# A long-convolution and feed-forward kernel: transposes in the network as products with the identity, in two halves of 64 output columns

## The chip, the cores and the metric

The kernel runs on one NeuronCore of a Trainium2 chip. The metric is the device time of one execution in microseconds. A TensorE (PE) instruction pair is one weight load (LDWEIGHTS, shown as PEld) and one product (MATMUL, shown as PE); VectorE is DVE, ScalarE is ACT, GpSimd is POOL.

## The reference

Everything is float32. The first part gates `x` with a long causal convolution of `x * v`; the second is a two-layer network on the 49920 rows that come out.

```python
# B, S, D = 4, 12480, 128
h_mlp = np.maximum(pos_emb @ w1, 0.0) @ w2
h_filt = h_mlp * np.exp(-0.01 * np.arange(S))[:, None]
u = x * v
L = 2 * S
y = irfft(rfft(u, L, axis=1) * rfft(h_filt, L, axis=0)[None], L, axis=1)[:, :S]
rows = (x * y).reshape(B * S, D)
h = rows @ w_in            # w_in 128 x 2048
g = h * np.cos(h)
out = g @ w_out            # w_out 2048 x 128
```

## The kernel before

**Start.** The filter is built, the transforms of the filter and of the first batch are made, and `w_in` and `w_out` are brought into their working form. The transforms are products with tables of sines and cosines in two stages, of 96 and 120 points; `f1`, `f2` and `i1`, `i2` are the forward and inverse stages in the names of the functions.

**The network and the convolution, interleaved.** From line 1114 on (`tiled[0] = True`) one order, written out by hand, mixes two streams on every engine. One stream is the network: 98 tiles (`NALL`) of up to 512 rows each, and per tile 16 chunks (`NFC`) of 128 hidden columns. The other is the convolution of the batches, a generator from which `convolve()` takes a step about once in a chunk; it makes the rows that the network later reads. After about 2970 us only the network is left.

**A chunk.** `moe_up` multiplies the tile's transposed input `at` with a chunk of `w_in` into a PSUM bank `ph` (three of them). ACT (L870), DVE (L871), ACT (L876) and DVE (L877) make `h * cos(h)` of it in `gt`. For two chunks together POOL makes sums of the parts (`ts`, L885 to L889), so that seven products take the place of eight in `moe_down` (L902), which runs seven chunks behind (`LAG = 7`) and adds into the accumulators `acca` and `accb`.

**A tile's transposes.** There are eight in a tile, all issued at chunk `AT = 10` (at the start and the end of the network the groups stand alone).

- `moe_back` takes the sums `ot` of the tile before, as `moe_evict` left them, and turns four blocks of 128x128 into a `ph` bank; `moe_rows` copies that bank to SBUF on ACT (L937), and `moe_store` sends it out.
- `moe_turn` takes the rows `zb` of the next tile (shown in the trace as `tile`), as `moe_load` brought them in, and turns four blocks of 128x128 into a bank of the convolution (`cv`, three banks, two while the first batch lasts); ACT copies it to `at` (L857).

In the order of PE they follow one another: a `moe_down`, then in many tiles a step of the convolution, the four of `moe_back`, the four of `moe_turn`, and then a `moe_up`.

**Two forms on TensorE.** `mm` (L135) issues every product of the network and of the convolution's later stages. Once `tiled[0]` is set it cuts a product in two at output column `CB = 64`, so that one half of the array's columns makes output partitions 0 to 63 and the other half 64 to 127. The products of `moe_down` (L902) and `f1_mm` (L458) are cut in the same way by hand. `transpose` (L140) does not use `mm`: it issues the transposing form over all 128 columns, with the data as the stationary operand and the identity as the moving one. `filter_turn` at the start uses it too, before `tiled[0]` is set.

The tile framework derives the waits between engines from the tiles that are written and read; the order on each engine is the order of issue.

Of the kernel before, what the change touches and what calls it, by code (L numbers as in the profile page):

```python
# [34 lines left out]
def kernel(  # L35
# [46 lines left out]
    nc = tc.nc  # L82
# [50 lines left out]
    tiled = [False]  # L133

    def mm(dst, left, right, start=True, stop=True):  # L135
        n = dst.shape[0]
        for lo, hi in ((0, CB), (CB, n)) if tiled[0] else ((0, n),):
            nc.tensor.matmul(dst[lo:hi], left[:, lo:hi], right, start=start, stop=stop)  # L138

    def transpose(dst, src, ident):  # L140
        n = src.shape[0]
        nc.tensor.transpose(dst, src, ident[0:n, 0:n])  # L142


    def float32_begin(pool, raw):
# [230 lines left out]
    def filter_turn(pool, bank, pe, ident):  # L376
        pt = bank()
        for q in range(ROWS // 2):
            transpose(pt[:, q * 2 * H:(q + 1) * 2 * H], pe[:, q, :], ident)
        peT = pool.tile([P, ROWS * H], F32, name="peT", bufs=3)  # L380
        nc.scalar.copy(out=peT[:, :], in_=pt[:, 0:ROWS * H])
        return peT
# [467 lines left out]
    def moe_turn(pool, n):  # L850
        m = rows_of(n)
        zb = zbs.pop(n)
        pt = bank()
        for i in range(G):
            transpose(pt[:, i * m:(i + 1) * m], zb[0:m, i, :], ident)
        at = pool.tile([D, BANK], F32, name="at")
        nc.scalar.copy(out=at[:, 0:G * m], in_=pt[:, 0:G * m])  # L857
        ats[n] = at
# [67 lines left out]
    def moe_back(n, ot):  # L926
        m = rows_of(n)
        pt = ps_h.tile([P, BANK], F32, name="ph")
        places = pt[:, :].rearrange("p (h i e d) -> p h e i d", h=2, e=2, d=CB)
        for i, block in enumerate((1, 2, 3, 0)):  # L930
            transpose(places[0:m, i // 2, i % 2], ot[:, block, 0:m], ident)
        return pt
# [21 lines left out]
    with tc.manual_schedule():  # L954
        with tc.tile_pool(name="psum", bufs=8, space=PSUM) as psum, \
# [15 lines left out]
            with tc.tile_pool(name="layers", bufs=1, side="right") as pool:  # L971
# [31 lines left out]
                ident = pool.tile([P, P], F32, name="ident")  # L1003
# [68 lines left out]
            ident = wpool.tile([P, P], F32, name="ident")  # L1072
# [61 lines left out]
        for i in range(len(steps) + LAG):  # L1134
# [5 lines left out]
            if i < len(steps):  # L1140
                n, c = steps[i]
# [55 lines left out]
```

## Time and profile before

| | |
|---|---|
| median of 3 runs | 3618.33 us (3617.26 to 3621.39) |
| profiled execution, device time | 3616.25 us |
| its span | 3614.5 us |
| PE busy | 3567.7 us, 99% of the span |
| DVE, POOL, ACT busy | 2836.4, 2752.1, 2234.2 us (78%, 76%, 62%) |
| mean share of DMA engines | 26.2% for the main queue |
| granted TensorE clock | 0.999 of full |
| transposes in the network (L142) | 784: 392 into `ph`, 392 into `cv` |
| chain that ended last | PE 84%, DVE 4%, POOL 2% |

A float32 product is recorded as two LDWEIGHTS and MATMUL pairs, so a product cut in two halves leaves four MATMUL records; a transpose in the transposing form leaves one. Matmuls are pipelined: a record lasts longer than the distance to the next one's start, so costs on PE are read from starts, not from durations. A line of the order-of-time view gives the start in us, the time from the first start to the last end of a run of like instructions, engine, line, operation, tiles written and read, shape, and the count of records.

### The profile page before, as it was taken

Reading aid. Unit: us, or ns where it says so; the run is one execution under the profiler, and the core shown is the slowest. Engines: PE = TensorE matmul, PEld = TensorE weight load, DVE = VectorE, ACT = ScalarE, POOL = GpSimd, SP = SyncE. Lnnn points to the kernel's source line nnn. Section 1 sums busy time; section 2 is a strip of 40 time slices with the busy share of each in tenths; the row PEclk is TensorE's granted clock in tenths of the full one; section 3 lists DMA queues with packets and bytes.
Section 4 is the critical chain, followed back from the end, with each engine's and each line's share of the span. In section 5 each row is a group of like instructions: output and inputs, shape, how many; then the busy total and the mean of one; then the engine's idle time right before and its main releaser. Section 6 shows DMA issues by size and latency. Waiting matters only on the chain.

```text
span 3614.5 us, 102269 instructions
## 1 busy us (share of the span) xinstructions
PE 3567.7 (99%) x40830; PEld 2533.1 (70%) x40830; DVE 2836.4 (78%) x5289; ACT 2234.2 (62%) x4482; POOL 2752.1 (76%) x3240
## 2 busy tenths in 40 slices
PE   8999999999999999999999999999999999999999
PEld 7996767666677767666677776766667776666666
DVE  7888885688887885688887786588887667877877
ACT  7776766666654556665655556665655446676676
POOL 7777985688855895698864897588885458878877
PEclk9999999999999999999999999999999999999999
DMA  6545530122214640122202551022220350000000
GB/s 189 157 147 169 159 114 16 35 72 70 70 35 130 171 134 13 31 71 72 76 26 68 171 171 47 13 65 72 74 63 15 109 153 19 19 25 19 19 23 17
DMA packets 224195, 281.85 MB, mean 78 GB/s; under 512 B 23386, under 2 KB 161122, under 8 KB 223594
## 3 DMA queue, kind: packets, MB, share of 16 engines
q1 hardware_dynamic: 223722, 275.30, 26.2%
q8 instruction: 326, 5.34, 0.6%
q14 instruction: 147, 1.20, 0.1%
HBM read 194.75 MB, written 80.46 MB: 76 GB/s over the span
## 4 chain that ended last, share of the span: by engine, by line
PE 84%; DVE 4%; POOL 2%; issue 1%; ACT 1%; DMA 0%; POOLq 0%; ACTq 0%; SPq 0%; DVEq 0%
PE ph L138 31%; PE accb L902 17%; PE cv L138 17%; PE acca L902 13%; PE cv L458 3%; DVE gt L871 1%; DVE gt L877 1%; PE ph L142 1%; PE cv L142 1%; ACT gt L870 1%; POOL ts L885 1%; POOL slots L450 0%; POOL ts L888 0%; DVE t L517 0%; DVE xt L440 0%
## 5 line engine op out<-in xcount | busy, mean ns | idle before, releaser
L871 DVE SCALAR_TENSOR_TENSOR gt<-ph,gt 128x512 f32<-128x512 f32 (+1 forms) x1380 | 948.9, 688 | 680.0 <-ACT gt L870 674.9
L870 ACT ACTIVATE gt<-ph 128x512 int32<-128x512 f32 (+1 forms) x1380 | 822.8, 596 | 1056.7 <-PE ph L138 992.6
L138 PE MATMUL ph<-at,w_in_sb 128*64 128x512 f32 (+1 forms) x5520 | 1429.0, 593 | 7.7 <-DVE gt L877 6.1
L885 POOL TENSOR_TENSOR ts<-gt 128x512 f32<-128x512 f32 (+2 forms) x784 | 1001.3, 1277 | 569.8 <-PE accb L902 565.6
L876 ACT ACTIVATE gt<-gt 128x512 f32<-128x512 f32 (+1 forms) x1568 | 972.3, 620 | 6.7 <-DVE gt L871 5.3
L877 DVE TENSOR_TENSOR gt<-ph,gt 128x512 f32<-128x512 f32 (+1 forms) x1380 | 936.6, 679 | 0.0
L902 PE MATMUL accb<-ts,w_out_sb 128*64 128x128 f32 (+2 forms) x9408 | 650.0, 272 | 0.0
L889 POOL TENSOR_TENSOR ts<-gt,ts 128x256 f32<-128x256 f32 (+2 forms) x784 | 575.7, 734 | 61.5
L888 POOL TENSOR_TENSOR ts<-ts,gt 128x256 f32<-128x256 f32 (+2 forms) x784 | 575.5, 734 | 61.4
L902 PEld LDWEIGHTS acca<-gt,w_out_sb 128*64 128x64 f32 x6272 | 395.4, 136 | 262.9 <-issue 228.6
L902 PEld LDWEIGHTS accb<-ts,w_out_sb 128*64 128x64 f32 x9408 | 543.7, 137 | 0.0
L902 PE MATMUL acca<-gt,w_out_sb 128*64 128x128 f32 (+2 forms) x6272 | 477.8, 272 | 0.0
L902 PEld LDWEIGHTS accb<-gt,w_out_sb 128*64 128x64 f32 x3136 | 221.4, 136 | 251.7 <-issue 198.7
L138 PEld LDWEIGHTS ph<-at,w_in_sb 128*64 128x64 f32 x5520 | 345.9, 137 | 37.7 <-issue 17.7
L902 PE MATMUL accb<-gt,w_out_sb 128*64 128x128 f32 (+1 forms) x3136 | 310.5, 273 | 4.9 <-DVE ot L923 3.3
L138 PEld LDWEIGHTS cv<-slots,tm 96*40 96x40 f32 (+1 forms) x3840 | 226.4, 125 | 119.5 <-issue 112.3
L902 PE MATMUL acca<-ts,w_out_sb 128*64 128x128 f32 (+1 forms) x3136 | 307.5, 272 | 1.5 <-POOL ts L888 1.4
L518 POOL TENSOR_TENSOR slots<-slots,t 120x256 f32<-120x256 f32 x288 | 210.7, 733 | 72.8 <-DVE t L517 62.0
L138 PE MATMUL cv<-slots,tm 96*40 96x128 f32 (+1 forms) x3840 | 253.0, 273 | 3.4 <-DVE slots L564 3.4
L138 PEld LDWEIGHTS cv<-even,slots 120*64 120x64 f32 (+1 forms) x3072 | 165.7, 125 | 65.0 <-issue 60.2
L902 PEld LDWEIGHTS acca<-ts,w_out_sb 128*64 128x64 f32 x3136 | 200.4, 137 | 2.5 <-POOL ts L888 2.3
L138 PE MATMUL cv<-at,w_in_sb 128*64 128x512 f32 (+1 forms) x752 | 191.7, 586 | 0.0
(140 smaller groups left out, 3834.8 us busy)
## 6 DMA issues: line engine op xcount, KB each, us to landing
h<-hd SPq DMA_DIRECT2D x144, 240.0 KB
tm<-td SPq DMA_DIRECT2D x96, 312.0 KB
xt<-in_x_dram SPq DMA_DIRECT2D x120, 208.0 KB
xs<-in_x_dram SPq DMA_DIRECT2D x120, 208.0 KB
zd<-xs SPq DMA_DIRECT2D x119, 208.0 KB
tile<-zd SPq DMA_DIRECT2D x96, 256.0 KB
vt<-in_v_dram SPq DMA_DIRECT2D x90, 208.0 KB
w<-wd SPq DMA_DIRECT2D x144, 105.0 KB
```

Of the source, the lines that this page charges most:

```text
L138: nc.tensor.matmul(dst[lo:hi], left[:, lo:hi], right, start=start, stop=stop)
L142: nc.tensor.transpose(dst, src, ident[0:n, 0:n])
L458: nc.tensor.matmul(dst[lo:hi], u[:, b, lo:hi, i], c1[0:u.shape[0], r:r + 2, :].rearrange("p r k -> p (r k)"), start=True, stop=True)
L518: nc.gpsimd.tensor_tensor(y[:, r], y[:, r], t[:, r], op=op)
L870: nc.scalar.activation(turns, ph[:, 0:m], AF.Identity, bias=phase)
L871: nc.vector.scalar_tensor_tensor(out=part, in0=ph[:, 0:m], scalar=phase, in1=turns, op0=ALU.add, op1=ALU.subtract)
L876: nc.scalar.activation(part, part, AF.Sin, scale=scale)
L877: nc.vector.tensor_tensor(part, ph, part, op=ALU.mult)
L885: nc.gpsimd.tensor_tensor(ts[:, 0:2, 0:half], gt[:, :, half:2 * half], gt[:, 0, 0:2 * half].rearrange("p (h n) -> p h n", h=2), op=ALU.sub ...
L888: nc.gpsimd.tensor_tensor(t[2], t[1], b11, op=ALU.add)
L889: nc.gpsimd.tensor_tensor(t[3], b21, t[2], op=ALU.subtract)
L902: nc.tensor.matmul(acc[h * CB:(h + 1) * CB, place, 0:r], w_out_sb[:, pair, weight, :], right[:, h * r:(h + 1) * r], start=(pair == 0 and i ...
```

## The change

In the network (when `tiled[0]` is set) `transpose` calls `mm` with the same data as the stationary operand and the same identity as the moving one. The product is cut at output column 64 as all others. Before the network, in `filter_turn`, the transposing form stays. Nothing else is touched: the order, the banks and the copies on ACT are the same.

```diff
     def transpose(dst, src, ident):
         n = src.shape[0]
-        nc.tensor.transpose(dst, src, ident[0:n, 0:n])
+        if tiled[0]:
+            mm(dst, src, ident[0:n, 0:n])
+        else:
+            nc.tensor.transpose(dst, src, ident[0:n, 0:n])
```

## The prediction

> **What bounds the kernel now.** I read the page first: the shares by engine and the chain that ended last.
>
> ```profile
> span 3614.5 us, 102269 instructions
> PE 3567.7 (99%) x40830; PEld 2533.1 (70%) x40830; DVE 2836.4 (78%) x5289; ACT 2234.2 (62%) x4482; POOL 2752.1 (76%) x3240
> ...
> PE 84%; DVE 4%; POOL 2%; issue 1%; ACT 1%; DMA 0%; POOLq 0%; ACTq 0%; SPq 0%; DVEq 0%
> ```
>
> PE is the bound: 99% busy, 84% of the chain. A busy PE is not yet a PE without slack, so I asked for busy times by stage, and show a stage in which the convolution's products with the spectrum run beside the network (690 to 1010 us, one of three alike) and the last one, network alone.
>
> ```profile
> 690.00:1010.00 320.00, 318.31 (x3352) 202.46 (x3350) 277.52 (x547) 192.79 (x352) 282.09 (x332) 1.00 0.24 69
> 2970.00:3572.00 602.00, 600.75 (x6503) 388.58 (x6503) 477.38 (x792) 419.35 (x769) 482.70 (x528) 1.00 0.07 21
> ```
>
> The columns are the length, then busy us of PE, PEld, DVE, ACT and POOL, the granted clock, the DMA share and GB/s. PE is without idle time in both. In the first, DVE (277.5 of 320) and POOL (282.1 of 320) are near it, 87 and 88%; in the second they are at 79 and 80%. So a microsecond added to PE is a microsecond of the span, but for places where PE waits today for DVE. Those I looked for last, in the groups of the transposes by form.
>
> ```profile
> L142 PE MATMUL ph<-ident,ot 128*128 128x128 f32 x384 | 62.9, 286 | 1.0 <-DVE gt L877 1.0
> L142 PE MATMUL cv<-ident,tile 128*128 128x128 f32 x384 | 58.2, 274 | 6.8 <-DVE t L517 4.2 <-PE ph L142 1.5 <-issue 1.1
> ```
>
> 384 records are 96 tiles of four: one record for each transpose. Ahead of `moe_turn`'s four PE sat idle 6.8 us in the whole run, mostly for a `cv` bank that DVE's L517 still read.
>
> **The change, step by step.** The cost comes from starts in the order of time on PE, here around one tile's eight transposes.
>
> ```profile
> 2018.33 0.61 PE L902 MATMUL acca<-gt,w_out_sb 128*64 128x128 f32 x8
> 2018.77 0.39 PE L902 MATMUL acca<-ts,w_out_sb 128*64 128x128 f32 x4
> 2018.99 1.03 PE L138 MATMUL ph<-at,w_in_sb 128*64 128x512 f32 x4
> 2019.84 1.07 PE L138 MATMUL cv<-slots,tm 96*64 96x128 f32 x16
> ...
> 2025.18 0.82 PE L902 MATMUL accb<-ts,w_out_sb 128*64 128x128 f32 x12
> 2025.93 0.66 PE L142 MATMUL ph<-ident,ot 128*128 128x128 f32 x4
> 2026.42 0.60 PE L142 MATMUL cv<-ident,tile 128*128 128x128 f32 x4
> 2026.95 1.08 PE L138 MATMUL ph<-at,w_in_sb 128*64 128x512 f32 x4
> 2027.86 0.61 PE L902 MATMUL acca<-gt,w_out_sb 128*64 128x128 f32 x8
> ```
>
> *Price of a product in halves.* The first two lines: 8 records from 2018.33 to 2018.77, 4 more to 2018.99. Four records are one product with 128 moving columns in two halves, so it takes 0.22 us of PE; the median over all runs of four such L902 starts is 0.218. L902 is as near as a row can be: 128 contracted rows, 64 output columns a half, 128 moving columns, new float32 weights for each. The convolution's 96-row product takes the same (16 records in 0.91 us at 2019.84, 0.22 each), so the rows do not set the price. The new transpose is this product: eight in a tile take 8 x 0.218 = 1.744 us.
>
> *What is taken out.* Eight transposes from 2025.93 to 2026.95: 1.02 us. Inside a group they start 0.109 us apart, half the product's price. But the group also pays at its edges. The twelve L902 records should hold PE for 3 x 0.218 = 0.654 us, to 2025.83; the first transpose starts at 2025.93: 0.10 us lost. Of the 1.02 us, 8 x 0.109 = 0.87 is streaming, and the other 0.15 lies after the first and the last transpose. The `ph` product behind takes 0.91 us (2026.95 to 2027.86) where the one at 2018.99 takes 0.85 to 0.86: 0.05 lost. So the eight cost 0.10 + 1.02 + 0.05 = 1.17 us, of which 0.30 is the price of going from halves to the whole array and back. Is that 0.30 the array's, or a wait that would stay? In 22 of the tiles the first transpose waits for no semaphore at all, and its start still stands 0.20 us behind the last L902 start, where 0.10 to 0.11 is usual. So I take it to go away with the form.
>
> The Trainium skill, "TensorEngine Tiling (Array Packing)", section Tiling Modes, says that changing the tiling mode drains TensorE. The 0.30 us agrees with it, and by that rule alone the change would be a gain of 98 x 0.30 = 29 us. The same skill's "Perfetto Trace Analysis", section Transposes, says that a transpose should use the transposing form and not an ordinary matmul; the steps of 0.218 against 0.109 us agree with that. The rows price both, and the second is the larger.
>
> *Net for a tile with PE at work throughout:* 1.744 - 1.17 = +0.575 us. 96 tiles: +55.2 us. Four groups stand alone (two `moe_turn` at the start, two `moe_back` at the end): 4 x 0.218 - (4 x 0.109 + 0.30) = +0.14 us each, 0.6 together. Sum +55.8 us.
>
> *What hides some of it.* Where PE waits at `moe_turn`'s bank, a longer `moe_back` eats the wait:
>
> ```profile
> 761.32 0.64 PE L138 MATMUL cv<-slots,w 124*64 124x256 f32 x4
> 761.88 0.66 PE L142 MATMUL ph<-ident,ot 128*128 128x128 f32 x4
> 762.97 0.66 PE L142 MATMUL cv<-ident,tile 128*128 128x128 f32 x4 [0.43 <-DVE t L517]
> 763.56 1.08 PE L138 MATMUL ph<-at,w_in_sb 128*64 128x512 f32 x4
> ```
>
> Here the second group starts 1.09 us after the first, not 0.49. With products the first group starts 0.10 earlier and takes 0.872, so it is done 0.77 after today's start: of the 0.60 us of waiting 0.28 is eaten. Counting in the order of time, 18 of the 96 paired blocks take over 1.1 us in place of 1.02: 18 x 0.27 = 4.9 us at most. The seven tiles from 280 to 540 us stand in a stage where PE is idle 10 us for other waits too (DVE's L877 ahead of `ph`); there I let the other 0.29 us be hidden as well: 2 us. Bounds: nothing hidden, 0; all of PE's idle time in the network hidden, by stages 10 (280 to 540 us), 14 (540 to 3572) and 6 (the end), 30 us. I take 7, near the lower end, because the waits that the trace names at these blocks are that small.
>
> *What comes at no cost.* ACT waits for the longer groups (L857, L937) and everything queued behind it on ACT (the next L870, L876) moves back by the same 0.58 us; but PE's next `ph`, which feeds them, moves back as much, so no bank comes later relative to PE. DVE and POOL get 0.58 us of slack in each tile. If that cover failed and ACT's lag came back to PE in full, it would cost as much again, 0.58 us a tile or 55 us; today's waits show PE held by ACT at `ph` once, for 0.6 us. Weight loads: four of 64 columns for one of 128. L902 streams the same load per product at 0.218 us, so they are inside that price. No DMA is added; 784 x 3 = 2352 more pairs, 5.8% of PE's 40830, come with the same density as L902's.
>
> *Sum.* 55.8 - 7 = +48.8 us on the profiled execution's 3616.25 (span 3614.5 and 1.75 around it). The median of the runs, 3618.33, lies 2.08 higher; I add to that: 3667.
>
> **Rivals.**
>
> *A gain: one pass is enough.* The transposing form leaves one record and starts every 0.109 us; if a product with the identity also went at 0.109 us, only the 0.30 us of switching would be left of the account: 98 x -0.30 = -29 us, 3589. The point of decision is a price per product of 1.17 / 8 = 0.146 us. For it: the switch is real, and the transposing form shows that a 128-column pass can start every 0.109 us. Against it: every L902 product with 128 columns leaves four records at 0.218, and no row of a float32 product with 128 moving columns is near 0.146. 5%.
>
> *The switch price stays.* If the 0.30 us came from the banks changing hands or from waits on PE's own semaphore, and not from the form, the change costs 0.30 x 98 = 29 us more: 3697. For it: 24 of the first transposes wait for PE's own semaphore. Against it: the 22 that don't wait. Half of the ACT lag above coming back to PE would give the same time. 6%.
>
> *The halves do not run side by side.* Then a product costs 0.436, a tile 8 x 0.436 - 1.17 = +2.3 us, 228 in all: 3846. Against it: L902's and L138's halves start 5 ns apart throughout, and L138's use one moving operand for both halves, as here. 2%.
>
> *More is hidden than I count,* up to the 30 us: 3644. For it: DVE and POOL at 87 and 88% in three stages, which the slack lets catch up. Against it: the order of time shows PE's waits at the transposes in 18 tiles alone, and in the last 600 us, 22 tiles, PE has nothing to hide behind. Values down to 3654 belong to my forecast, below that 5%.
>
> **Chances and range.** Forecast, slower by about 49 us: 82%, with 3654 (20 us hidden) to 3674 (nothing hidden) as its own ends. The rest as above. The range reaches from 3654 past the uncovered sum towards the case in which a third of the switch price stays (10 us): 3654 to 3684. A measurement of this kernel can tell 0.2%, 7 us, from no change. Slower by over that: all but the gain and a sliver left for the unforeseen, 0.94; within it 0.01; faster 0.05.
>
> **What would show it.** Right: L142 `ph` and `cv` records in the network become four for each transpose, 64 columns wide, at 0.218 us a transpose; the block of eight takes 1.74 us; the first starts 0.10 to 0.11 us after the last L902 record; the `ph` product behind takes 0.86; the last stage, 22 tiles, grows by 22 x 0.575 = 12.6 us; PE's idle time at `moe_turn` shrinks. Wrong: groups of eight at under 1.17 us (the gain), a start 0.20 us behind L902 as today (the switch stays), or starts of the two halves 0.1 us apart (no overlap).

## The result and the profile after

The median is 3669.40 us (3668.72 to 3670.05, four runs) against 3619.24 us before (3617.26 to 3621.39, four runs): 50.2 us slower, a ratio of 1.0138 (95% interval 1.0121 to 1.0156). The profiled execution took 3668.97 us, its span 3667.2 us, 52.7 us above the span before. Three parts of the page say where PE stands: its head, the shares by engine, and the chain that ended last.

```profile
span 3667.2 us, 106973 instructions
PE 3626.0 (99%) x43182; PEld 2690.7 (73%) x43182; DVE 2827.2 (77%) x5289; ACT 2224.6 (61%) x4482; POOL 2748.6 (75%) x3240
...
PE 86%; DVE 4%; POOL 1%; ACT 1%; issue 1%; DMA 0%; ACTq 0%; POOLq 0%; DVEq 0%
```

PE is busy 58.3 us longer, with 2352 more MATMUL records; DVE, ACT and POOL do the same work in a longer span. The transposes of the network now belong to `mm` (L138), here in the groups by form:

```profile
L138 PE MATMUL ph<-ident,ot 128*64 128x128 f32 x1552 | 105.0, 273 | 1.5 <-DVE gt L880 1.0 <-DVE ot L926 0.4
L138 PE MATMUL cv<-ident,tile 128*64 128x128 f32 x1536 | 102.8, 273 | 4.1 <-issue 2.2 <-DVE t L520 1.3 <-PE ph L138 0.6
```

1536 records are 96 tiles of four transposes of four records each; the `ph` form holds 16 more, the first halves of the short tiles. Idle time ahead of `moe_turn`'s group fell from 6.8 to 4.1 us, the part that DVE ended from 4.2 to 1.3. The order of time on PE shows the same tile that the prediction took apart, `moe_back`'s group first:

```profile
2050.00 0.39 PE L905 MATMUL accb<-gt,w_out_sb 128*64 128x128 f32 x4
2050.22 0.82 PE L905 MATMUL accb<-ts,w_out_sb 128*64 128x128 f32 x12
2050.87 1.04 PE L138 MATMUL ph<-ident,ot 128*64 128x128 f32 x16
2051.74 1.04 PE L138 MATMUL cv<-ident,tile 128*64 128x128 f32 x16
2052.62 1.03 PE L138 MATMUL ph<-at,w_in_sb 128*64 128x512 f32 x4
2053.47 0.39 PE L905 MATMUL acca<-gt,w_out_sb 128*64 128x128 f32 x4
```

Starts 2050.87, 2051.74 and 2052.62 make four transposes 0.87 us, 0.218 each. The first starts 0.65 us behind the twelve L905 records, which is what these take; the 0.10 us of before is gone. The `ph` product takes 0.85 us, not 0.91.

The tile that waited for `moe_turn`'s bank:

```profile
767.43 1.05 PE L138 MATMUL ph<-ident,ot 128*64 128x128 f32 x16
768.64 1.09 PE L138 MATMUL cv<-ident,tile 128*64 128x128 f32 x16 [0.16 <-DVE t L520]
```

The second group starts 1.21 us after the first, and 0.87 of that is work: 0.34 us of waiting is left of the 0.60 before.

**A finer measure.** Where the network runs alone, the distance from one tile to the next repeats to a few ns, so a price can be read there without the noise of whole runs. I take it from the starts of ACT's copy into `at`; two of them after the change are

```profile
3205.32 0.59 ACT L860 COPY at<-cv 128x512 f32<-128x512 f32 x1 [1.50 <-PE cv L138]
3233.29 0.59 ACT L860 COPY at<-cv 128x512 f32<-128x512 f32 x1 [1.50 <-PE cv L138]
```

27.97 us apart; before the change the median of twenty is 27.411, after it 27.971, +0.560 us. The experiments below are compared by this, beside their medians.

### The profile page after: what moved, and what is told of

Same layout as the page of the kernel before. It is cut to its first block, busy times and chain, and to the rows that moved or that the text cites. A ratio compares the mean times of both kernels' runs of the same rounds, so it can differ in the third digit from the quotient of the medians.

```text
span 3667.2 us, 106973 instructions
## 1 busy us (share of the span) xinstructions
PE 3626.0 (99%) x43182; PEld 2690.7 (73%) x43182; DVE 2827.2 (77%) x5289; ACT 2224.6 (61%) x4482; POOL 2748.6 (75%) x3240
## 4 chain that ended last, share of the span: by engine, by line
PE 86%; DVE 4%; POOL 1%; ACT 1%; issue 1%; DMA 0%; ACTq 0%; POOLq 0%; DVEq 0%
PE ph L138 33%; PE cv L138 19%; PE accb L905 17%; PE acca L905 13%; PE cv L461 3%; DVE gt L874 1%; DVE gt L880 1%; ACT gt L873 1%; POOL ts L888 0%; POOL slots L453 0%; DVE t L520 0%; DVE xt L443 0%; POOL ts L891 0%; DVE slots L518 0%; DVE slots L567 0%
## 5 line engine op out<-in xcount | busy, mean ns | idle before, releaser
L138 PE MATMUL ph<-at,w_in_sb 128*64 128x512 f32 (+1 forms) x5520 | 1444.5, 592 | 5.1 <-DVE gt L880 4.1
L905 PE MATMUL accb<-ts,w_out_sb 128*64 128x128 f32 (+2 forms) x9408 | 661.2, 272 | 0.0
L905 PEld LDWEIGHTS acca<-gt,w_out_sb 128*64 128x64 f32 x6272 | 417.2, 136 | 244.2 <-issue 214.2
L905 PEld LDWEIGHTS accb<-ts,w_out_sb 128*64 128x64 f32 x9408 | 554.8, 137 | 0.0
L905 PE MATMUL acca<-gt,w_out_sb 128*64 128x128 f32 (+2 forms) x6272 | 490.5, 272 | 0.0
L905 PEld LDWEIGHTS accb<-gt,w_out_sb 128*64 128x64 f32 x3136 | 240.5, 136 | 235.7 <-issue 186.8
L138 PEld LDWEIGHTS ph<-at,w_in_sb 128*64 128x64 f32 x5520 | 370.4, 137 | 18.2 <-DVE gt L880 7.7
L905 PE MATMUL accb<-gt,w_out_sb 128*64 128x128 f32 (+1 forms) x3136 | 321.8, 273 | 4.1 <-DVE ot L926 2.8
L905 PE MATMUL acca<-ts,w_out_sb 128*64 128x128 f32 (+1 forms) x3136 | 320.1, 272 | 1.3 <-POOL ts L891 1.2
L138 PEld LDWEIGHTS cv<-slots,tm 96*40 96x40 f32 (+1 forms) x3840 | 227.9, 125 | 120.2 <-issue 112.4
L138 PE MATMUL cv<-slots,tm 96*40 96x128 f32 (+1 forms) x3840 | 254.2, 273 | 4.4 <-DVE slots L567 3.4
L905 PEld LDWEIGHTS acca<-ts,w_out_sb 128*64 128x64 f32 x3136 | 212.9, 137 | 2.3 <-POOL ts L891 2.1
L138 PEld LDWEIGHTS cv<-even,slots 120*64 120x64 f32 (+1 forms) x3072 | 165.7, 125 | 65.0 <-issue 60.1
L461 PEld LDWEIGHTS cv<-c,slots 104*64 104x64 f32 (+1 forms) x1536 | 140.9, 137 | 85.0 <-issue 66.6
```

The lines of the kernel that those rows point to most:

```text
L461: nc.tensor.matmul(dst[lo:hi], u[:, b, lo:hi, i], c1[0:u.shape[0], r:r + 2, :].rearrange("p r k -> p (r k)"), start=True, stop=True)
L905: nc.tensor.matmul(acc[h * CB:(h + 1) * CB, place, 0:r], w_out_sb[:, pair, weight, :], right[:, h * r:(h + 1) * r], start=(pair == 0 and i ...
```

## The experiments

The theory: PE sets the time; a product costs 0.218 us, a transposing form 0.109, and going from halves to the whole array and back costs 0.30 us once for a block. The change pays the first difference eight times and saves the last once. Rivals: the edges cost nothing, or belong to the transposing form and not to the width, or the forecast was met by errors that cancel.

**1. Products over the whole array** (`e1_whole`)

```diff
         if tiled[0]:
-            mm(dst, src, ident[0:n, 0:n])
+            nc.tensor.matmul(dst, src, ident[0:n, 0:n], start=True, stop=True)
```

> Transposes as ordinary products with the identity, but over all 128 output columns, not in two halves. Theory (0.30 us at the edges of a tile's block is the price of going from halves to the whole array and back, whatever the form): the edge price stays and each transpose costs 0.218 us in place of 0.109, so +0.87 us a tile; 27.41 us a tile in the network's last stage becomes 28.28; 85 us in all, some 7 hidden, about 3697 us against 3619 before. Rival (the edge price belongs to the transposing form): as the changed kernel, 27.97 us a tile, about 3669 us.

3703.78 us, ratio to before 1.0239 (1.0222 to 1.0256); 28.367 us a tile. The order of time on PE in the last stage:

```profile
3316.40 0.85 PE L905 MATMUL accb<-ts,w_out_sb 128*64 128x128 f32 x12
3317.18 1.16 PE L143 MATMUL ph<-ident,ot 128*128 128x128 f32 x8
3318.18 1.06 PE L143 MATMUL cv<-ident,tile 128*128 128x128 f32 x8
3319.16 1.08 PE L138 MATMUL ph<-at,w_in_sb 128*64 128x512 f32 x4
3320.07 0.61 PE L905 MATMUL acca<-gt,w_out_sb 128*64 128x128 f32 x8
```

The edges are back with no transposing form in the block: the twelve records hold PE for 0.655 us, and the first product starts 0.78 us behind their start; `ph` takes 0.91. So the price goes with the width of the array, and the rival falls. The kernel is 7 us slower than expected, 0.085 us a tile: inside a group the products start every 0.223 us, not 0.218, and the second record of the block starts 0.21 us behind the first, 0.05 more than in the kernel before.

**2 and 3. One of the two groups alone** (`e2_back_only`, `e3_turn_only`)

```diff
-    def transpose(dst, src, ident):
+    def transpose(dst, src, ident, halves=False):
...
-        if tiled[0]:
+        if halves:
             mm(dst, src, ident[0:n, 0:n])
...
# e2: halves=True in moe_back's call; e3: in moe_turn's
```

> Only moe_back's four transposes become products in halves; moe_turn's keep the transposing form. Theory: the array still goes to the whole width and back once in a tile, so the 0.30 us stays and four transposes cost 0.109 more: +0.436 us a tile, 27.85 us in the last stage; 42.7 us in all, less about 6 that the longer first group hides of the waits for moe_turn's bank: about 3655 us. Rival (no price at the edges, the cost simply goes with the number of products): half of the 50 us, 27.69 us a tile, about 3644 us.

> Only moe_turn's four transposes become products in halves; moe_back's keep the transposing form. Theory: +0.436 us a tile, 27.85 us in the last stage, 42.7 us in all, and since the longer group comes behind the wait for the bank, little is hidden (up to 2 us): about 3660 us, some 5 more than with moe_back alone; the two together exceed the whole change's 50 us by the price of one change of width, about 28 us. Rival (no price at the edges): half of the 50 us, about 3644 us.

3654.57 us (ratio 1.0103, 1.0088 to 1.0118) and 3656.75 us (1.0110, 1.0095 to 1.0125), against 3617.27 us of the kernel before beside them: +37.3 and +39.5. In the last stage 27.846 and 27.849 us a tile, +0.435 and +0.438, where the rival gave 27.69. The parts add to 0.873, the whole change is 0.560: 0.313 us a tile is paid by each part and not by the whole, the change of width. Of the order between the two by what is hidden, the medians show 2 us where 5 were expected, which is within their intervals (some 5 us to each side). The single traces agree better: the last copy into `at` stands 37.1 us later than before in e2 and 41.1 in e3.

**4. The two groups apart, in the transposing form** (`e4_apart`)

```diff
-                if c == (AT if n else NFC - 2) and n + 1 < NALL:
-                    moe_turn(mpool, n + 1)
                 ...
                 hidden[i] = moe_up(mpool, n, c, pairs[i - c % 2], ph)
+                if c == (AT if n else NFC - 2) and n + 1 < NALL:
+                    moe_turn(mpool, n + 1)
```

> The kernel before, with moe_turn's four transposes issued behind the chunk's moe_up, so that a product in halves lies between the two groups: twice from halves to the whole array and back in a tile. Theory: +0.30 us a tile, 27.71 us in the last stage (22 tiles, +6.6 us); in all +29 us less up to 10 us of waits for moe_turn's bank that the later place avoids: 3638 to 3648 us. Rival (the edges cost nothing, the place alone counts): the last stage stays at 27.41 us a tile and the run at 3609 to 3619 us.

3671.30 us, ratio 1.0150 (1.0135 to 1.0165): the last stage as expected, 27.711 us a tile, exactly +0.300; the whole run 54 us slower where 19 to 29 were expected. From tile 8 to 12 (553 to 699 us before) a tile cost +0.50 us, from tile 12 to 22 (699 to 1018) +0.71. ACT in order of time, between 553 and 699 us, suggests a cause:

```profile
593.63 0.59 ACT L937 COPY tile<-ph 128x512 f32<-128x512 f32 x1 [2.06 <-PE cv L142]
594.11 0.60 ACT L870 ACTIVATE gt<-ph 128x512 int32<-128x512 f32 x1
594.60 0.59 ACT L857 COPY at<-cv 128x512 f32<-128x512 f32 x1
595.07 0.65 ACT L876 ACTIVATE gt<-gt 128x512 f32<-128x512 f32 x1
```

and PE beside it:

```profile
591.29 0.66 PE L142 MATMUL ph<-ident,ot 128*128 128x128 f32 x4
591.88 1.08 PE L138 MATMUL ph<-at,w_in_sb 128*64 128x512 f32 x4
592.89 0.66 PE L142 MATMUL cv<-ident,tile 128*128 128x128 f32 x4
593.48 0.66 PE L902 MATMUL acca<-gt,w_out_sb 128*64 128x128 f32 x8
593.97 0.39 PE L902 MATMUL acca<-ts,w_out_sb 128*64 128x128 f32 x4
594.27 1.08 PE L138 MATMUL ph<-at,w_in_sb 128*64 128x512 f32 x4
```

L937 copies the bank that `moe_back` filled by 591.95, yet it starts at 593.63, released by `moe_turn`'s group on `cv`. It writes `tile`, the one buffer that also holds the rows which `moe_turn` reads. All that is queued behind it on ACT waits too. PE's next `ph` product, due 0.22 us after 593.97, starts at 594.27, 0.08 us late and just behind the end of L937 (593.63 + 0.59), which still read one of the three `ph` banks. In the waits by pairs, PE's `ph` behind DVE's L877 rose from 6.1 to 21.0 us. Two runs were made to test this reading: one that leaves ACT alone, one that takes the shared buffer away.

**5. A second change of width with nothing moved on ACT** (`e9_back_early`)

```diff
         for i in range(len(steps) + LAG):
+            if i < len(steps):
+                n, c = steps[i]
+                if c == AT and n - 1 in ots:
+                    turned[n - 1] = moe_back(n - 1, ots.pop(n - 1))
             if i >= LAG:
                 ...
-                if c == AT and n - 1 in ots:
-                    turned[n - 1] = moe_back(n - 1, ots.pop(n - 1))
```

> The kernel before with moe_back's four transposes ahead of the chunk's moe_down (and of the convolution's step), moe_turn's where they were: again two changes of width and back in a tile, but this time nothing moves on ACT. Theory (the second change costs 0.30 us; what the apart kernel cost above that was a lag of ACT): 27.71 us a tile in the last stage and also about 0.30 us a tile where the convolution's first stage runs (553 to 699 us), +29 us in all, and up to 7 more because moe_turn's bank is asked for 0.49 us earlier: 3647 to 3654 us. Rival (the second change costs 0.5 us where the convolution runs): 0.50 us a tile in 553 to 699 us, about 3670 us.

3646.78 us, ratio 1.0080 (1.0063 to 1.0097), +29.0 us over 3617.81; 27.713 us a tile in the last stage, and +0.31 a tile from tile 8 to 12. One change of width and back is worth 98 x 0.30 = 29 us. The up to 7 us more do not show in the total, but the match is partly luck: from tile 12 to 22 (the table below) a tile cost 0.45 us. There PE waited 3.1 us at `moe_back`'s `ph` bank for DVE's L877, where the kernel before waited 1.2 us at `moe_turn`'s bank. The tiles outside the table's stages stood at 0.27 on average.

**6. Apart, with a buffer of its own for the rows that go out** (`e10_apart_own`)

```diff
# on top of e4_apart
-                t = pool.tile([R, 2, UA * D], F32, name="xv"[i] + "t", bufs=3 - i)
+                t = pool.tile([R, 2, UA * D], F32, name="xv"[i] + "t", bufs=2)
...
-        ob = pool.tile([P, G, D], F32, name="tile", bufs=1)
+        ob = pool.tile([P, G, D], F32, name="ob", bufs=1)
```

> The apart kernel with a buffer of its own for the rows that moe_rows copies out (it shared one buffer with the rows that moe_turn reads, so that ACT's L937 had to wait for moe_turn's transposes); to make room, the loads of x for the next batch have two buffers in place of three, so the stage of the last inverse steps (1172 to 1383 us) may change for that reason. Theory (apart's excess is ACT's L937 waiting for moe_turn): in 553 to 699 us +0.30 to +0.35 us a tile in place of apart's 0.50, in 699 to 1018 us under apart's 0.71; 3645 to 3658 us. Rival (the excess comes from elsewhere, such as L857 ahead of the sine on ACT): 0.50 and 0.71 us a tile as before, about 3670 us.

3754.20 us, ratio 1.0383 (1.0367 to 1.0399): the buffer taken from the loads of `x` cost 100 us in the stages that use it, far more than I allowed for, and the whole run answers nothing. The waits by pairs on PE name 70 us of that price, at the loads of `tm`, an operand of the convolution that is read in the same stages:

```profile
PE cv L138 <- DMA tm<-td: 69.8, 31, 6.2
PE ph L138 <- DVE gt L877: 16.0, 38, 1.9
```

Where these loads do not run, the stages can still be read:

| added to a tile, us | tiles 8 to 12 | 12 to 22 | 35 to 45 | 59 to 69 | 76 to 96 |
|---|---|---|---|---|---|
| the change | 0.56 | 0.52 | 0.44 | 0.48 | 0.56 |
| e4, apart | 0.50 | 0.71 | 0.65 | 0.70 | 0.30 |
| e9, back early | 0.31 | 0.45 | 0.31 | 0.29 | 0.30 |
| e10, apart, own buffer | 0.37 | 0.39 | 0.36 | 0.36 | 0.30 |

With its own buffer L937 starts before `moe_turn` is done, and of e4's excess over 0.30 us, 0.20 and 0.35 to 0.41 a tile, 0.07 and 0.06 to 0.09 are left. The shared buffer is most of it; the rest was not taken apart.

**7 and 8. Every transpose twice** (`e5_twice_before`, `e6_twice_after`)

```diff
# e5, on the kernel before
-        nc.tensor.transpose(dst, src, ident[0:n, 0:n])
+        for _ in range(2 if tiled[0] else 1):
+            nc.tensor.transpose(dst, src, ident[0:n, 0:n])
# e6, on the changed kernel
-            mm(dst, src, ident[0:n, 0:n])
+            for _ in range(2):
+                mm(dst, src, ident[0:n, 0:n])
```

> The kernel before with every transpose of the network issued twice in succession, in the transposing form: eight more transposes a tile and no more changes of width. Theory: the form's own price is 0.109 us, so +0.87 us a tile, 28.28 us in the last stage, 85 us in all, some 6 of it hidden: about 3698 us. Rival (the transposing form carries its drain with it at each transpose, and the edges are only where it shows): 1.17 / 8 = 0.146 us each, +1.17 us a tile, 28.58, about 3728 us.

> The changed kernel with every transpose of the network issued twice in succession, as products in halves. Theory: 0.218 us each, +1.744 us a tile on the changed kernel's 27.97, 29.71 us in the last stage; 171 us over the changed kernel's 3669, some 6 hidden: about 3834 us. Rival (a product with the identity is cheaper than its neighbours, and the forecast was met by two errors that cancel): under 1.6 us a tile, under 29.57.

3695.70 us (1.0213, 1.0196 to 1.0230) and 3834.52 us (1.0597, 1.0581 to 1.0612). In the last stage 28.285 us a tile, 0.874 above the kernel before: 0.109 for each further transpose. And 29.721, 1.750 above the changed kernel: 0.219 each. Both unit prices stand by themselves, without an edge in them. So in the price of a tile no errors cancel, and both rivals (28.58, and under 29.57 us) fall.

**9 and 10. The groups in the other order** (`e7_swap_before`, `e8_swap_after`): `moe_turn` ahead of `moe_back`, on both kernels.

```diff
-                if c == AT and n - 1 in ots:
-                    turned[n - 1] = moe_back(n - 1, ots.pop(n - 1))
                 if c == (AT if n else NFC - 2) and n + 1 < NALL:
                     moe_turn(mpool, n + 1)
+                if c == AT and n - 1 in ots:
+                    turned[n - 1] = moe_back(n - 1, ots.pop(n - 1))
```

> The kernel before with moe_turn's group ahead of moe_back's. Theory: the wait for moe_turn's bank comes 0.49 us earlier in the order, so it grows by up to 0.49 us where there is one today (18 tiles) and shows in some more: up to 9 us slower, 3619 to 3630 us; the last stage stays at 27.41. Rival (the waits at these blocks have no part in the time): 3619 us.

> The changed kernel with moe_turn's group ahead of moe_back's. Theory: no longer first group stands ahead of the wait for the bank, so the 5 us that it hid come back: the difference to the kernel before in the same order is about 55 us, not 50; beside the changed kernel's 3669 it is 3 to 14 us slower. Rival (nothing was hidden there): the difference in this order is 50 us too.

3622.73 us (1.0013, 1.0003 to 1.0022) and 3680.12 us (1.0169, 1.0154 to 1.0184). On the kernel before, the other order costs 4.8 us, within the up to 9 expected; on the changed kernel about 11, within the 3 to 14. In this order the change costs 57.4 us by medians and 55.8 by spans (3677.9 against 3622.1), in the kernel's own order 50.2 and 52.7. Both differences point to something that the longer `moe_back` hides and that comes back when it no longer stands first. Whether it is 3 us, 7 or none, these medians don't settle: the intervals are some 6 us wide to each side. The waits inside the blocks, counted below, show the hiding better.

None of the ten beats the kernel before.

## Why the prediction was right

- **The price of a product,** 0.218 us from L902: measured 0.218 in the block and 0.219 by doubling. Two halves run side by side as in the neighbours. That halves start 5 ns apart throughout was read wrongly: in the new products, and in many of L902 before, the distance is under 20 ns in some and 30 to 50 in others, and a product takes 0.22 us with either.
- **The price of the transposing form,** 0.109 us: 0.109 by doubling.
- **The edges,** 0.30 us, taken to go away with the form: gone in the trace after; 0.300 by a second change of width in e4's and e9's last stage, 0.313 from the two groups alone. That it is the width and not the transposing form is shown by e1. The Trainium skill, "TensorEngine Tiling (Array Packing)", Tiling Modes, has the drain at a change of mode; the trace agrees and gives its size here.
- **The net for a tile,** +0.575 us: 0.560 where the network runs alone.
- **What is hidden,** 7 us: this term was mis-sized. The last copy into `at` stands 51.2 us later than before, against 96 x 0.560 = 53.8: 3 us hidden. At the blocks themselves the count was good. The mean paired block of before was 0.110 us above its median, 10.6 us over 96 tiles, and after 0.059, 5.7 us: 4.9 us eaten, as forecast. What failed is the assumption that all of it lasts and that 2 us more are hidden from 280 to 540 us. Over the eight tiles there the change fell only 1.5 us short of its full price, waits at the blocks included. And from 1172 to 1383 us six tiles cost 4.8 us in place of 3.4. The first of them alone cost 1.89 us, and the trace after shows 1.04 us of it as a wait for a load that the trace before does not have in this tile; the other five cost 0.58 us each. Waits for this load of 0.2 to 1.7 us stand in the same stage in e1 to e3 and e5 to e9 too, also where no product replaces a transpose (e7: 0.4 us); what makes the load late was not tried.

```profile
1201.12 1.11 PE L138 MATMUL cv<-slots,tm 96*64 96x128 f32 x16 [1.04 <-DMA tm<-td]
```

The bound of 30 us for all of PE's idle time was also added up too low: by the windows it is 10.7 us from 280 to 540 us, 16.9 (not 14) to 3572 and 5.9 at the end, 33 us.

- **The lone groups,** 0.14 us each: the end, behind the last copy into `at`, grew by 1.6 us where two such groups were counted at 0.3. The very last `moe_back`, before and after (the view gives a run the form of its first record), and the form that it contains:

```profile
3610.10 0.50 PE L142 MATMUL ph<-ident,ot 128*88 128x128 f32 x3 [0.89 <-DVE ot L923]
3661.21 2.12 PE L138 MATMUL ph<-ident,ot 128*64 128x128 f32 x12 [0.43 <-DVE ot L926]
L138 PE MATMUL ph<-ident,ot 128*24 128x128 f32 x8 | 1.6, 281 | 0.0
```

Three transposes took 2.12 us in place of 0.50. The last tile has 88 rows, so the cut at 64 leaves halves of 64 and 24 columns. In the trace's single records these two do not run side by side: the first record of the 24 starts 0.20 us behind the last of the 64, as the first transpose did behind L902 before, and a transpose takes 0.69 us. The first tile has 104 rows: there the halves of 64 and 40 columns start 8 ns apart (at 333.00 us), and four transposes take the usual 0.87 us. The end grew by 1.7 us in e2 too, which has the same last group, and not in e3. So for this one group the rival "the halves do not run side by side" came true; a cut elsewhere was not tried.

- **No cost through ACT.** PE's `ph` waited 5.1 us for DVE's last step after the change, 6.1 before. What this cover was worth e4 shows: moved by one product, the same groups sent a lag of ACT back to PE.
- **Sum:** 48.8 us forecast on the profiled execution, 52.7 measured there, 50.2 by medians. The cover was 4 us too large and the end 1 us too small, the price of a tile 1.4 us too high over the 96: the last error cancels part of the first two.

The rivals: one pass is enough (3589) falls by e6, halves not side by side (3846) by the starts, the switch price stays (3697) by the `ph` product's 0.85 us, more hidden (3644) by the 3 us above. Of these, e1 is the kernel in which the switch price does stay: 3704.

## What to carry to other kernels

Price an instruction on a pipelined engine by the distance between starts in the nearest like stream, and price the edges of its block apart: a cheaper instruction in another array width pays at both ends, here 0.30 us, or 2.75 of the 0.109 us that it saves each time. With eight in a block the transposing form was right, and each further place where such a block stands alone costs another 29 us in this kernel. When a block is moved, look for buffers that two of its steps share under one name: the order of issue may be all that kept them from waiting. And when a product is cut at a fixed column, look at the short last tile by itself: its narrow rest may not run beside the other half.

## What was not expected of the hardware

A float32 product over all 128 output columns with new weights each time started every 0.223 us, while two halves side by side took 0.218, and it lost 0.05 us more at the first of a block (e1, 0.085 us a tile). The two halves were thus slightly cheaper than the whole array even without a change of width. And halves need not be equal but can be too unequal: 64 and 40 columns ran side by side, 64 and 24 did not (after, 0.218 against 0.69 us a transpose).
